# The order of the first 200 steps of a fused mLSTM and feed-forward kernel, rewritten

## The chip, the cores and the metric

One core of a Trainium2 chip runs the kernel. The metric is the device time of one execution in microseconds (us). The core has five engines that run side by side, each through its own list of instructions: PE (TensorE, matrix products), ScalarE (ACT in the profile), VectorE (DVE), GpSimd (POOL) and SyncE (SP), which here only issues DMAs.

## The reference

Two layers, one behind the other. The first is an mLSTM recurrence over 768 time steps for 4 batches and 8 heads of 40 channels; the second a feed-forward layer on the 3072 tokens.

```
for t in range(S):
    m_new = maximum(f[t] + m, i[t])
    f_stab, i_stab = exp(f[t] + m - m_new), exp(i[t] - m_new); m = m_new
    C = f_stab * C + i_stab * outer(v[t], k[t]);  n = f_stab * n + i_stab * k[t]
    y[t] = sigmoid(o[t]) * (C @ q[t]) / maximum(abs(n . q[t]), 1)
x = y as (3072, 320)
h = x @ w_in                                       # (3072, 2048)
g = where(h >= 1, h, where(h <= -1, 0, (h + 1)**2 / 4))
return g @ w_out                                   # (3072, 320)
```

## The kernel before

**Tiling.** The recurrence is computed in chunks of 128 time steps, 6 per batch, so 24 pieces numbered n = 0 to 23 (chunk n // 4, batch n % 4). Within a piece the recurrence is two matrix products per head: scores of k against q (`score.n`), multiplied by a 128x128 matrix of decays, then the product with the values (`main.n`). The state between chunks is made by `carry.n`. Four pieces give 512 tokens; for these the feed-forward layer runs in 16 blocks of 128 hidden channels: `mm` (x @ w_in, 8 matmuls of 512 columns), `relu`, `max`, then `out` (first blocks) or `outh` and `outl` into four PSUM sums, and `sto`.

**The order.** The whole program is a string, `STEPS` (line 48), read from left to right. Each word is one step of a kind with its number; a kind that is a generator goes on to its next yield each time it is named. Inside `STEPS` every instruction is tied to the one before it on the same engine, so the string is the order of each engine's instructions, SP's DMAs among them. What an engine doesn't wait for by its data it does in that order.

**The steps of the front.** They start the kernel before its streaming middle:

- `fi`, `fb`: DMAs of the gates: those of the first chunk, and two copies of those of chunks 1 to 4. `id`: the identity matrix (`ident`) and other constants. `cs`: a mask for `carry`.
- `sums.0`, `gtail.0`, `gex.0`: the gate sums of the first chunk on VectorE (tile `ac` and others, from `fi`), and one transposition on PE with exponentials on ScalarE (`G`).
- `mask.b`, `add.b`, `dec.b.h`: decays of the first chunk, batch b, made on PE: two 512-column matmuls write a mask into two PSUM banks, two groups of five add the sums, and ScalarE writes the exponentials of the two halves into the tile `Abc` (or `A`).
- `bmax.0` twice (a scan over 512 steps; then four DMAs that spread the maxima, `m_b<-m_r`), `bsum.0` three times, `btail.0` four times, `exps.0`, `decs.0` twice: the gates of chunks 1 to 4. `bsum.0`'s third part stores the sums to DRAM (`a_d`), from where `A.n` reads them back, spread over 128 partitions; `prep.n` then makes decays of them (POOL's selection, ScalarE's exponentials).
- `qk.n`: two DMAs of q and k (160 KB each). `vv.n`: values of two pieces (324 KB and a little more in tile `ow`); `v.n`, `qn.n`, `og.n`: values with k, q in another layout, output gates of a chunk. `v1.n`, `v2.n`: values times gates on POOL. `sig.n`: the sigmoid of the output gates on ScalarE, which loads another function table for it and back.
- `W.k`: DMA of the k-th piece of the weights, w_in (768 KB) and w_out (640 KB) in turn. `w.k`: its conversion, in five parts for w_in (ScalarE, ScalarE, VectorE, ScalarE, VectorE: tiles `mg`, `win`, `wh`, `wl`), three for w_out.
- `hot.k`: k matmuls of 512 columns on a tile of zeros, whose result nobody reads (filler).
- `score.n`: 16 passes on PE, then VectorE multiplies each half with the decays. `main.n` for n below 4: 16 passes (decayed scores times values), the denominators `z`, `y` times sigmoid, three transposes, two copies.

PSUM has eight banks of 512 columns, and the steps that need one take one that is free.

Setup ahead of `STEPS` (zeros, identity and mask in bf16) is the same in both versions.

Of the kernel before, what the change touches and what calls it, by code (L numbers as in the profile page):

```python
# [45 lines left out]


STEPS = (
    "fi.0 mask.1 fb.0 W.0 vv.0 mask.0 hot.2 sums.0 mask.3 qk.1 add.1 hot.2 add.0 qk.2 w.0 w.0 bmax.0 id.0 dec.1.0 "
    "dec.1.1 dec.0.0 score.1 qk.3 gtail.0 hot.2 hot.2 bmax.0 gex.0 score.1 mask.2 qk.0 add.2 dec.2.0 dec.2.1 vv.2 "  # L50
    "add.3 v.4 dec.3.1 v1.1 dec.3.0 score.1 og.0 W.1 dec.0.1 score.2 main.1 score.0 bsum.0 bsum.0 bsum.0 w.0 "
    "score.3 score.2 score.2 one.0 score.0 v.1 score.0 v1.2 btail.0 w.0 v1.0 sig.0 main.1 btail.0 hot.4 btail.0 "
    "btail.0 w.0 v1.3 main.0 score.3 v.0 main.0 W.2 hot.2 exps.0 main.0 main.1 main.2 hot.2 hot.2 qn.5 A.4 score.3 "
    "v2.4 main.2 main.2 main.0 w.1 v2.1 qk.4 main.0 w.1 cs.0 main.3 main.1 main.2 main.0 W.3 v.5 carry.4 main.3 "
    "main.3 hot.2 v2.0 qn.4 main.1 decs.0 main.1 v.2 w.1 carry.1 main.3 A.5 A.6 main.2 w.2 carry.0 main.2 main.3 "
    "main.3 prep.4 carry.0 w.2 v1.4 prep.4 v2.5 score.4 w.2 prep.4 decs.0 W.4 carry.1 w.3 -- score.4 mm.0 relu.0 "
    "max.0 mm.1 w.2 main.4 w.2 relu.1 main.4 W.5 carry.5 W.6 carry.4 v2.2 w.3 w.3 main.5 main.5 prep.5 prep.5 "
    "score.4 carry.2 carry.2 max.1 mm.3 relu.3 prep.5 mm.2 w.4 carry.5 qk.5 prep.6 main.4 relu.2 main.4 v1.5 max.3 "
    "w.4 w.4 carry.5 prep.6 w.5 qk.6 og.1 max.2 out.0 out.1 out.2 w.5 w.5 w.4 w.4 score.5 so.1 score.5 score.5 A.7 "
    "W.7 score.6 w.6 carry.4 carry.4 v.6 w.6 prep.7 score.6 prep.6 mm.5 w.6 score.6 v1.6 qn.6 sig.1 main.5 main.4 "  # L60
    "main.4 so.2 relu.5 so.2 max.5 main.5 mm.4 relu.4 w.6 main.5 w.6 qn.7 w.7 w.7 prep.7 out.3 main.6 main.6 main.6 "
    "v2.6 carry.6 max.4 mm.6 carry.5 w.7 gh.5 gl.5 carry.6 gh.4 so.3 so.3 v.3 v2.3 carry.3 W.8 outh.4.2.3 carry.6 "
    "w.8 w.8 mm.7 outh.4.0.1 gl.4 main.6 outl.4 outh.5.2.3 A.8 relu.6 carry.3 main.7 A.9 qk.7 score.7 w.8 main.5 "
# [965 lines left out]
```

## Time and profile before

| | |
|---|---|
| median of 3 runs | 466.06 us |
| the three runs | 465.94, 466.06, 479.42 us |
| the profiled execution, its own time | 465.84 us |
| its span in the profile | 464.1 us |
| PE busy | 456.0 us (98% of the span), 3333 matmuls |
| VectorE, ScalarE, POOL busy | 350.7, 327.5, 144.1 us |
| read and written in DRAM | 55.96 and 4.01 MB |

The span is the time from the first to the last instruction in the profile; 1.74 us of the execution's time lie around it. Times in the rows below count from the span's start. A matmul's duration is longer than the distance to the next one's start, because matmuls overlap; the distances tell what PE can do.

### The profile page before, as it was taken

How to read it: one execution, taken by the hardware profiler on the slowest of the kernel's cores; microseconds unless marked ns; L12 is line 12 of the kernel's file. 1: busy time of each engine (PE TensorE's matmuls, PEld its weight loads, DVE VectorE, ACT ScalarE, POOL GpSimd, SP SyncE). 2: the span in 40 equal slices, each digit the busy share in tenths (PEclk: the TensorE clock that was granted, in tenths of full speed). 3: DMA queues.
4: the chain of work that ended last, by engine and by line, in shares of the span. 5: the costliest groups of instructions: out<-in, count | busy, mean ns of one | idle time of the engine just before them, and what ended most of it. 6: DMA issues, size and time to landing. Idle time of an engine off the chain costs nothing.

```text
span 464.1 us, 8795 instructions
## 1 busy us (share of the span) xinstructions
PE 456.0 (98%) x3333; PEld 408.5 (88%) x3336; DVE 350.7 (76%) x625; ACT 327.5 (71%) x593; POOL 144.1 (31%) x153
## 2 busy tenths in 40 slices
PE   6999999999999999999999999999999999999996
PEld 3888789998899999999988899989988898989986
DVE  5786789998979889878999988786775985443523
ACT  3679999998985586877777666766777734464651
POOL 2364233212543624423425643433213231000000
PEclk9999999999999999999999999999999999999999
DMA  6899959726445442564165437234616000010001
GB/s 215 291 283 352 296 175 347 220 67 166 147 115 148 118 132 91 171 177 124 48 177 161 118 89 203 63 78 155 159 57 160 1 1 0 2 42 16 1 0 57
DMA packets 23048, 60.60 MB, mean 131 GB/s; under 512 B 2599, under 2 KB 9535, under 8 KB 23007
## 3 DMA queue, kind: packets, MB, share of 16 engines
q1 hardware_dynamic: 22719, 59.81, 43.2%
q8 instruction: 26, 0.43, 0.4%
q10 hardware_dynamic: 288, 0.25, 0.2%
q14 instruction: 15, 0.12, 0.1%
HBM read 55.96 MB, written 4.01 MB: 129 GB/s over the span
## 4 chain that ended last, share of the span: by engine, by line
PE 87%; DVE 4%; ACT 3%; DMA 3%; issue 1%; SPq 1%; DVEq 0%
PE ps L189 87%; DMA qs<-in_qs 1%; DMA ident<-in_cst 1%; ACT r L189 1%; DVE stk L189 1%; SPq L189 1%; DVE hv L189 1%; DVE r L189 1%; DVE gl L189 0%; ACT Abc L189 0%; ACT raw L189 0%; ACT win L189 0%; ACT mg L189 0%; DVE win L189 0%; DVE xl L189 0%
## 5 line engine op out<-in xcount | busy, mean ns | idle before, releaser
L189 PE MATMUL ps<-oh,gh 128*128 128x320 f32 x368 | 112.3, 315 | 0.1
L189 PE MATMUL ps<-ow,gh 128*128 128x320 f32 x368 | 110.1, 309 | 0.0
L189 PE MATMUL ps<-xh,wh 128*128 128x512 f32 x288 | 100.6, 403 | 0.1
L189 PE MATMUL ps<-xh,wl 128*128 128x512 f32 x288 | 98.2, 395 | 0.0
L189 ACT ACTIVATE r<-ps,half 128x512 f32<-128x512 f32 x96 | 65.6, 683 | 44.5 <-PE ps L189 39.4
L189 DVE SCALAR_TENSOR_TENSOR r<-ps,r 128x512 f32<-128x512 f32 x96 | 64.7, 685 | 39.0 <-ACT r L189 38.7
L189 DVE TENSOR_TENSOR gl<-r,gh 128x512 fp32r<-128x512 f32 x92 | 69.9, 769 | 25.7 <-ACT gh L189 24.7
L189 ACT CAST gh<-r 128x512 fp32r<-128x512 f32 x92 | 56.2, 617 | 46.4 <-PE ps L189 21.6
L189 PEld LDWEIGHTS ps<-oh,gh 128*128 128x128 f32 x368 | 69.1, 188 | 1.9 <-issue 0.3
L189 PEld LDWEIGHTS ps<-ow,gh 128*128 128x128 f32 x368 | 69.2, 188 | 1.3
L189 PE MATMUL ps<-oh,gl 128*128 128x320 f32 x368 | 70.2, 311 | 0.0
L189 PEld LDWEIGHTS ps<-xh,wl 128*128 128x128 f32 x288 | 54.1, 188 | 12.8
L189 ACT ACTIVATE r<-r 128x512 f32<-128x512 f32 x96 | 60.7, 633 | 3.0
L189 PE MATMUL ps<-xl,wh 128*128 128x512 f32 x192 | 60.3, 395 | 0.0
L189 PEld LDWEIGHTS ps<-oh,gl 128*128 128x128 f32 x368 | 58.1, 188 | 1.1
L189 PEld LDWEIGHTS ps<-xh,wh 128*128 128x128 f32 x288 | 50.3, 188 | 7.8 <-DVE Abc L189 0.2
L189 ACT ACTIVATE Abc<-Abc,nA 128x128 f32<-128x128 f32 x160 | 50.4, 391 | 0.1
L189 POOL TENSOR_TENSOR v<-vk,G 128x328 f32<-128x328 f32 x36 | 28.9, 807 | 53.2 <-DMA vk<-in_vk 28.2
L189 POOL TENSOR_TENSOR y<-y,z 128x320 f32<-128x320 f32 x24 | 21.1, 882 | 76.2 <-DVE y L189 76.2
L189 PEld LDWEIGHTS ps<-xl,wh 128*128 128x128 f32 x192 | 36.0, 188 | 8.8
L189 POOL TENSOR_TENSOR m<-m 128x1024 bf16<-128x1024 f32 x16 | 31.6, 1976 | 37.6 <-DVE m L189 35.0
L189 DVE SCALAR_TENSOR_TENSOR stk<-raw,ident,qs 120x1024 fp32r<-120x1024 f32 x28 | 37.9, 1356 | 2.9 <-ACT raw L189 2.8
(143 smaller groups left out, 665.4 us busy)
## 6 DMA issues: line engine op xcount, KB each, us to landing
qs<-in_qs SPq DMA_DIRECT2D x28, 480.0 KB
Abc<-a_d SPq DMA_DIRECT2D x20, 512.0 KB
vk<-in_vk SPq DMA_DIRECT2D x20, 324.0 KB
wraw<-in_w_in SPq DMA_DIRECT2D x8, 768.0 KB
wraw<-in_w_out SPq DMA_DIRECT2D x8, 640.0 KB
sig<-in_og SPq DMA_DIRECT2D x6, 640.0 KB
qn<-in_qn SPq DMA_DIRECT2D x20, 180.0 KB
raw<-in_qk SPq DMA_DIRECT2D x20, 160.0 KB
```

What stands on the lines that cost most here:

```text
L189: r = getattr(self.engine, name)(*args, **kwargs)
```

## The change

The first 204 words of `STEPS` are put into another order. They are the same words, each as often as before; from `mm.5` (near the end of the last changed line) both lists are the same. No function changes. In the new list `sums.0`, `gtail.0` and `add.1` come right behind the gate DMAs, `id.0`, `vv.0`, the first `bmax.0` and `qk.1` stand ahead of `W.0`; the other masks, the scores, the fillers and the loads behind them move with respect to each other.

```diff
 STEPS = (
-    "fi.0 mask.1 fb.0 W.0 vv.0 mask.0 hot.2 sums.0 mask.3 qk.1 add.1 hot.2 add.0 qk.2 w.0 w.0 bmax.0 id.0 dec.1.0 "
-    "dec.1.1 dec.0.0 score.1 qk.3 gtail.0 hot.2 hot.2 bmax.0 gex.0 score.1 mask.2 qk.0 add.2 dec.2.0 dec.2.1 vv.2 "
-    "add.3 v.4 dec.3.1 v1.1 dec.3.0 score.1 og.0 W.1 dec.0.1 score.2 main.1 score.0 bsum.0 bsum.0 bsum.0 w.0 "
-    "score.3 score.2 score.2 one.0 score.0 v.1 score.0 v1.2 btail.0 w.0 v1.0 sig.0 main.1 btail.0 hot.4 btail.0 "
-    "btail.0 w.0 v1.3 main.0 score.3 v.0 main.0 W.2 hot.2 exps.0 main.0 main.1 main.2 hot.2 hot.2 qn.5 A.4 score.3 "
-    "v2.4 main.2 main.2 main.0 w.1 v2.1 qk.4 main.0 w.1 cs.0 main.3 main.1 main.2 main.0 W.3 v.5 carry.4 main.3 "
...
+    "fi.0 mask.1 fb.0 sums.0 gtail.0 add.1 dec.1.0 dec.1.1 id.0 hot.2 vv.0 bmax.0 mask.3 mask.0 gex.0 qk.1 v1.1 W.0 "
+    "w.0 w.0 add.3 hot.2 one.0 score.1 score.1 add.0 dec.0.0 score.1 qk.0 w.0 w.0 dec.0.1 main.1 bmax.0 bsum.0 "
+    "score.0 score.0 v1.0 dec.3.1 mask.2 og.0 sig.0 hot.4 bsum.0 qk.3 score.0 main.0 qk.2 vv.2 v1.2 w.0 add.2 "
+    "dec.2.0 dec.2.1 main.1 main.0 score.3 W.1 bsum.0 W.2 score.2 main.1 dec.3.0 score.2 score.2 v1.3 qk.4 hot.2 "
+    "btail.0 hot.2 hot.2 main.2 main.0 hot.2 v.1 v2.1 score.3 main.0 score.3 v.0 btail.0 btail.0 cs.0 w.1 main.3 "
+    "w.1 w.1 v.2 score.4 carry.1 main.0 btail.0 decs.0 hot.2 main.3 main.1 w.2 w.2 main.2 main.2 v2.0 main.0 main.3 "
+    "main.1 v2.2 carry.1 A.4 prep.4 main.1 hot.2 main.2 main.2 carry.0 carry.0 exps.0 qn.5 v.4 main.2 v2.4 main.5 "
+    "qn.4 W.3 decs.0 main.5 main.3 main.3 A.5 prep.5 main.3 w.2 carry.2 v1.4 main.4 prep.4 score.4 prep.4 score.4 "
...
```

## Rows read from the trace of the kernel before

**Rows 1.** Busy us by windows: length, PE, PEld, VectorE, ScalarE, POOL, clock, DMA share, GB/s.

```profile
0.00:12.07 12.07, 8.11 (x49) 4.28 (x51) 7.21 (x24) 4.41 (x6) 3.10 (x15) 1.00 0.66 212
12.07:53.52 41.45, 41.30 (x330) 34.90 (x332) 30.52 (x68) 33.48 (x66) 17.61 (x22) 1.00 0.97 312
53.52:464.10 410.58, 406.63 (x2955) 369.35 (x2955) 312.95 (x535) 289.64 (x522) 123.36 (x117) 1.00 0.38 110
```

**Rows 2.** Timeline, PE: start us, us, engine, line, operation, out<-in, shape, count.

```profile
2.18 0.58 PE L186 MATMUL ps<-late_t,idb 128*128 128x512 bf16 x1 [2.18 <-POOL rst L186]
2.56 1.49 PE L189 MATMUL ps<-late_t,idb 128*128 128x512 bf16 x3
3.84 1.06 PE L189 MATMUL ps<-zeros 128*128 128x512 bf16 x2
...
5.59 0.39 PE L189 MATMUL ps<-ac,pick 96*128 96x128 bf16 x4
...
6.47 0.59 PE L189 MATMUL ps<-zeros 128*128 128x512 bf16 x2
...
9.02 0.46 PE L189 MATMUL ps<-raw 40*128 40x128 f32 x2 [1.07 <-DMA raw<-in_qk]
...
14.51 1.16 PE L189 MATMUL ps<-raw 40*128 40x128 f32 x16
15.60 1.98 PE L189 MATMUL ps<-ow,Abc 128*128 128x41 f32 x16
...
22.52 0.27 PE L189 MATMUL ps<-ident,fi_b 128*128 128x128 f32 x1
...
22.95 1.88 PE L189 MATMUL ps<-ow,Abc 128*128 128x41 f32 x16
24.66 1.03 PE L189 MATMUL ps<-zeros 128*128 128x512 bf16 x4
25.53 0.49 PE L189 MATMUL ps<-ident,y 128*128 128x128 f32 x3
...
53.52 0.70 PE L189 MATMUL ps<-xh,wh 128*128 128x512 f32 x2
```

**Rows 3.** Timeline, ScalarE, 6 to 24 us; in brackets the idle time before.

```profile
6.95 0.90 ACT L186 ACTIVATE mg<-wraw 128x768 f32<-128x768 f32 x1 [4.93 <-DMA wraw<-in_w_in]
...
8.53 1.55 ACT L189 ACTIVATE Abc<-ps 128x512 f32<-128x512 f32 x3
...
21.25 1.27 ACT L189 ACTIVATE sig<-sig 128x1280 f32<-128x1280 f32 x1 [1.68 <-DMA sig<-in_og]
22.54 1.28 ACT L189 ACT_TABLE_LOAD   x1
```

**Rows 4.** Timeline, VectorE, 9 to 18 us.

```profile
9.19 0.14 DVE L189 COPY carry<-m_r 32x1 f32<-32x1 f32 x1
11.01 1.29 DVE L189 TENSOR_TENSOR Abc<-ps,Abc 128x512 f32<-128x512 f32 x2 [1.67 <-PE ps L189]
14.75 0.62 DVE L189 TENSOR_TENSOR fi_b<-fi_b,m_b 128x128 f32<-128x128 f32 x2 [2.46 <-DMA m_b<-m_r]
...
16.45 0.95 DVE L189 SCALAR_TENSOR_TENSOR win<-mg,win 128x768 int32<-128x768 int32 x1
```

**Rows 5.** Timeline, DMA issues on SP, 0 to 24 us.

```profile
2.56 0.43 SPq L189 DMA_DIRECT2D wraw<-in_w_in  x1
...
7.98 3.37 SPq L189 DMA_DIRECT2D m_b<-m_r  x4
...
14.25 0.42 SPq L189 DMA_DIRECT2D sig<-in_og  x1
...
16.38 0.33 SPq L189 DMA_DIRECT2D a_d<-fi_r  x1
...
23.05 0.33 SPq L189 DMA_DIRECT2D Abc<-a_d  x1
```

**Rows 6.** Timeline, POOL, at 31 us: the selection of piece 4.

```profile
30.89 1.09 POOL L189 TENSOR_SCALAR_AFFINE_SELECT Abc<-Abc 128x1024 f32<-128x1024 f32 x1
```

10 rows, old and new, of the table STEPS are left out of this document.

## The prediction

> **What bounds the kernel now.** I read the page's busy shares first (PE 98%), then the busy time by windows cut where the changed part of the list ends. The first `mm.5` matmul, the first work behind the changed steps, starts at 53.52 us [rows 2]. In the 410.6 us from there PE is busy 406.6 us, and nothing in them is reordered; in 12.07 to 53.52 it is busy 41.30 of 41.45 us [rows 1]. So TensorE's own work sets the time, and the change can only alter how early PE reaches `mm.5`. The time that PE doesn't use lies almost wholly in the first 12.07 us, where it is busy 8.11 us, part of that at half speed [rows 1]. Next I read the timelines of that stretch engine by engine. They show three things. PE starts at 2.18 us, and its 512-column matmuls start 0.43 us apart up to about 5.2 us, against 0.22 us later: (3.84 - 2.56) / 3 against (25.53 - 24.66) / 4 [rows 2]. That is 1.2 and 2.4 GHz; the granted-clock column says 1.00 throughout and doesn't show it. Second, PE waits: `score.1` begins at 9.02 after 1.07 us for a piece of q and k that queues behind the first piece of w_in [rows 2]. Third, ScalarE runs the first two conversion steps from 6.95 before it makes the first decays at 8.53 [rows 3].
>
> **The yardstick.** After the same steps, `main.2` starts its first real product (call it up.2; up.0 and up.1 are those of batches 0 and 1). Up to it both lists hold the same PE steps (four masks, 14 filler matmuls, four `add`, four scores, `gex`, up.1, up.0), but the old list has `exps.0` as well. Old: up.2 starts at 22.95 and `exps.0` took 22.52 to 22.95 [rows 2], so the shared work was done at 22.52. The new list's start of up.2 minus 22.52 is the change, as long as nothing later stalls.
>
> **Removed.** Both lists start `add.1` at 5.59 us, since it hangs on the gate sums on VectorE, which are not moved. From there to 22.52 are 16.93 us. Prices by start-to-start [rows 2]: `add` 0.88 (5.59 to 6.47), a score 1.09 (14.51 to 15.60), an up 1.71 (22.95 to 24.66), a filler or half mask 0.22, a transpose 0.11 (four in 0.43). The old list's work in that stretch is 4 x 0.88 + 4 x 1.09 + 2 x 1.71 + 12 fillers and 2 half masks at 0.217 (3.04) + 0.11 = 14.45 us. So 2.48 us there are waits, and they are what the change can take away: w_in's piece no longer stands ahead of q and k, and the first decays no longer stand behind its conversion.
>
> **Added, part 1: work that loses its place.** While the gate sums run, old PE does eight matmuls (three masks and two fillers); the new list has only the two of `mask.1` ahead of `add.1`. Six matmuls move behind 5.59: 6 x 0.217 = +1.30 us.
>
> **Added, part 2: the clock.** Old PE works without a break from 2.18, and by 5.59 it runs at 2.4 GHz. New PE works from 2.18 to about 3.1 and then stands for 2.5 us. No row shows PE after such a break. I take it that the lower level lasts as long after 5.59 as it does in the one stretch that the trace has (2.18 to about 5.2), so to about 8.7. What runs until then, `add.1`, two fillers and half a mask, takes double: +0.88 + 0.43 + 0.21 = +1.52 us. The bounds are 0 (full speed from 5.59) and 3.0 us (a stretch twice as long); I take 1.52, from the nearest row.
>
> The Trainium skill ("TensorE: Matmul & The Clock Gate", Part 1: The HAM clock gate) says that the array idles at half rate, that activity lifts it, and that the point of the rise differs from run to run of one kernel. The trace agrees with half rate at the start; one profile can't show the spread. By that page the term may come out as nothing, and that is the first rival.
>
> **Added, part 3: two new gaps.** Step by step from 5.59: `add.1` to 7.35, fillers 8.20, `mask.3` 8.85, `mask.0` 9.28, `gex` 9.4, `add.3` 10.3, fillers 10.7, `score.1` 11.8, `add.0` 12.7. VectorE multiplies score 1 in two halves of 0.65 (11.01, [rows 4]), to 13.1, and only then can up.1 go: a gap of 0.4 us. up.1 to 14.8, `score.0` 15.9, `mask.2` 16.35, four fillers 17.2. VectorE multiplies score 0 from 15.95; the grid rounding of `bsum.0` (0.45) stands between its halves, so it ends at 17.7 and up.0 starts at 17.75: a gap of 0.55 us. up.0 to 19.45, `add.2` 20.35, `score.3` 21.45, `score.2` 22.5, six fillers 23.8, while VectorE finishes score 2 at 23.85. up.2 starts at 23.85. Gaps: +0.95 us.
>
> **What hides the rest.** SP: ident, the first value block and the first q and k pieces are issued ahead of w_in's first piece, which leaves some 2 us later than 2.56 [rows 5]. It took 4.4 us to land [rows 3, 5], so it lands at 9 to 10.2; its two ScalarE steps (1.6 us) then end at 11.9 at the latest, and VectorE takes it at 13.1 (0.95 us, [rows 4]): covered by 1.2 us. The four copies that broadcast the maxima start when the long scan ends. The same VectorE instructions end at 9.33 in the old list [rows 4] and about 9.2 in the new one, so the copies leave at 9.2 instead of 7.98 and, with no q and k landings to wait for between them, take some 2.1 us instead of 3.37 [rows 5]. The old ones landed 3.4 us after the last issue (11.35 to 14.75 [rows 4, 5]); the new ones so by 14.7. VectorE's `bsum.0` reaches them at 14.2 and is done (0.6 us) ahead of score 0 at 15.95: nothing, and 0.6 us of cover. The 2.46 us that VectorE waited there before [rows 4] were no wait of PE's.
>
> **Sum** against the profiled execution's 465.84 us: -2.48 + 1.30 + 1.52 + 0.95 = +1.3, so 467.1. The median of the three runs, 466.06, lies 0.22 above that execution; with this the time is 467.3 us, +0.3%. A measurement of this kernel tells about 2% (9.3 us) from no change; all of PE's unused time in the changed part is less than that.
>
> **Rival 1: the clock is up in time.** Without the 1.52 us the walk gives up.2 at about 22.35 (gaps 1.0 us): -0.2, so 465.7 to 465.9. If both gaps closed as well, 15.77 us of work from 5.59 would give -1.16: 464.7, which is the floor, since no work is removed. For it: 0.9 us of early work. Against: a break nearly three times as long.
>
> **Rival 2: loads come late behind the sums' store.** `a_d` is written when VectorE has scanned the sums: new at about 20.5 (behind up.0's `z` step), old at 16.38 [rows 5]. On SP everything else queues behind it: `W.2`, q and k 4, four value blocks, `A.4`. `A.4` also waits until `a_d` has landed, old 6.7 us (16.38 to 23.05), and POOL's selection began 7.8 us after that (30.89) [rows 5, 6]. With both durations kept, the selection comes at 35.0 and `v2.4` behind it on POOL at 36.1, where `carry.4` on PE wants it at 35.3: 23.85 plus 11.4 us (two ups, score 4, six steps of six passes at 0.107, twelve transposes and the four of `exps.0`, six fillers). `qn.5` behind `A.4` on SP is wanted at about 33. That is a stall of 1.5 to 3 us: 468.8 to 470.3. Against: at 20.5 the queue holds little besides `W.1`, where the old `a_d` stood behind five loads, so both durations should shrink by some 2 us. It decides once `a_d` takes over 5 us to land. DMA engines are 0.97 busy in this whole stretch [rows 1], so lost time there doesn't come back.
>
> **Rival 3, slower: ScalarE stuck at the sigmoid.** In the new list `sig.0` stands ahead of the decays of batch 2 and of half of batch 3. `og.0` leaves SP behind the maxima at about 11.3. With the old 7.0 us (14.25 to 21.25) it lands at 18.3; sigmoid 1.27, table load 1.28, decays 0.52 each [rows 3], so batch 2's first is done at 21.4 (`add.2` ends at 20.35), and VectorE wants it at 22.55. The cover is 1.1 us. From 8.1 us of landing time each further one goes to score 2, up.2 and PE. With the time of one more piece of w_in in the queue (4.4 us), it is 3.3 us: 470.6. Past 2% (475) it would need 10 us, or it would have to make ScalarE, which is busy 33.5 of the 41.5 us from 12.07 to 53.52 [rows 1], late in what follows.
>
> The same skill ("DMA: Bandwidth & Descriptors", Anatomy of one DMA) gives a fixed cost of about 2.0 us and 436 GB/s beyond it. By that, an estimate, `og.0`'s 0.64 MB land 3.5 us after issue and rival 3 is gone; the trace's 7.0 us stands against it, so I keep the rival.
>
> **Chances.** Forecast 0.50; rival 1 0.23; rival 2 0.17; rival 3 0.08, of it 0.03 past 2%; not named 0.02. The range 464.6 to 470.3 reaches from rival 1's floor to the top of rival 2. Faster by over 2%: 0.01, since PE's work stays; within 2%: 0.95; slower: 0.04.
>
> **What would show it.** In the new profile: PE's 512-column matmuls after 5.59 start 0.43 apart to about 8.7; `add.1` at 5.6; `score.1` without a wait for q and k; up.1 at 13.1, up.0 at 17.75, up.2 near 23.9 and `mm.5` near 54.8; VectorE without a long wait for the maxima; from 53.5 us on the same spacing as before. It is wrong if up.2 starts before 22.5 or after 25.5, if PE stands in 24 to 55 us, or if the part behind `mm.5` changes its length by over 1 us, for which I have no term.

## The result, and the profile after

| | before | after |
|---|---|---|
| median (lowest to highest), 4 runs each | 466.09 us (465.94 to 479.42) | 471.31 us (470.83 to 472.01) |
| profiled execution, its span | 465.84, 464.1 us | 470.83, 469.0 us |
| first matmul of `mm.5` | 53.52 us | 58.14 us |
| behind it | 410.58 us | 410.86 us |

The new list is slower: the ratio is 1.0115, with a 95% interval of [1.0098, 1.0133]. That is 5.2 us, above the forecast (467.3) and above the range (470.3). Against the bound of 2% it is still "no change". Executions more than 1.5% above the fastest of the same kernel, such as the one of 479.42 us, are left out of every ratio and of every count of falls here.

Busy time by windows, with the same cuts as in [rows 1] and the same columns:

```profile
0.00:12.07 12.07, 7.52 (x51) 4.28 (x52) 6.08 (x22) 4.02 (x6) 4.94 (x18) 1.00 0.62 188
12.07:58.14 46.07, 44.65 (x332) 37.20 (x332) 32.26 (x72) 34.25 (x67) 16.84 (x19) 0.93 0.93 292
58.14:469.00 410.86, 406.96 (x2957) 369.55 (x2955) 310.93 (x532) 289.49 (x522) 122.20 (x116) 1.00 0.37 109
```

4.62 of the 4.9 us by which the span grew lie ahead of `mm.5`, as they had to. The second window has what the one of before had not: 1.42 us in which PE isn't busy, and a mean granted clock of 0.93. PE's timeline shows where:

```profile
5.56 0.58 PE L189 MATMUL ps<-ac,pick 96*128 96x128 bf16 x4 [2.36 <-DVE ac L189]
...
7.22 1.06 PE L189 MATMUL ps<-zeros 128*128 128x512 bf16 x2
8.07 1.32 PE L189 MATMUL ps<-late_t,idb 128*128 128x512 bf16 x4
...
10.75 1.16 PE L189 MATMUL ps<-raw 40*128 40x128 f32 x16
...
12.81 1.95 PE L189 MATMUL ps<-ow,Abc 128*128 128x41 f32 x16
...
17.09 1.87 PE L189 MATMUL ps<-ow,Abc 128*128 128x41 f32 x16
...
23.07 1.88 PE L189 MATMUL ps<-ow,Abc 128*128 128x41 f32 x16
...
27.35 1.16 PE L189 MATMUL ps<-raw 40*128 40x128 f32 x16
29.61 1.58 PE L189 MATMUL ps<-ow 128*120 128x123 f32 x6 [1.10 <-POOL ow L189]
31.00 1.23 PE L189 MATMUL ps<-fi_r 128*120 128x16 f32 x6
...
35.01 1.26 PE L189 MATMUL ps<-ow 128*120 128x123 f32 x6
...
37.51 0.79 PE L189 MATMUL ps<-ow 128*120 128x123 f32 x6
...
39.36 0.72 PE L189 MATMUL ps<-xh,wh 128*128 128x512 f32 x2
```

The opening runs as it was walked through: `score.1` at 10.75 has no wait, up.1 is at 12.81, up.0 at 17.09, up.2 at 23.07. Then at 29.61 PE has stood (had nothing that it could start) for 1.10 us in front of `carry.1`, for a product on POOL; its idle time and what ended it stand in brackets. From there six matmuls on `ow` take 1.58 us, and six of the same shape 0.79 at 37.51. The windows around it say what that is (the granted clock is the third column from the right):

```profile
25.00:29.00 4.00, 3.52 (x37) 3.20 (x35) 3.22 (x15) 2.38 (x4) 0.17 (x1) 1.00 1.05 288
29.00:30.00 1.00, 0.39 (x2) 0.39 (x3) 0.57 (x2) 0.00 (x0) 1.00 (x2) 0.57 1.02 337
30.00:35.00 5.00, 4.78 (x21) 3.99 (x22) 1.24 (x3) 0.48 (x1) 1.61 (x3) 0.50 1.06 279
35.00:36.00 1.00, 1.00 (x6) 1.00 (x6) 0.32 (x2) 0.48 (x1) 1.00 (x3) 0.52 0.98 339
36.00:40.00 4.00, 4.00 (x37) 3.91 (x36) 3.35 (x8) 3.22 (x12) 1.82 (x3) 1.00 1.03 320
```

While PE stands, TensorE's clock falls to 1.2 GHz, and it stays there until about 36 us although PE is at work again. What PE stood for is read from the chain that ended last (start us, us, what):

```profile
19.40 0.04 DVE z L189
19.44 0.08 issue
19.52 0.37 DVE fi_r L189
19.89 0.19 DVE fi_b L189
20.09 0.17 SPq L189
...
21.58 7.18 DMA ow<-in_vk
...
28.83 0.74 POOL ow L189
...
29.61 3.04 PE ps L189 x13
```

Read backwards: `carry.1` waits for `v2.1` on POOL, that for the value block `v.1`, whose DMA took 7.18 us from 21.58. It left so late because it stands on SP behind the store `a_d`, which waits for VectorE's scan of the sums (19.52), and that stands behind up.0's `z`. In the old list the store leaves at 16.38 [rows 5] and `v.1` directly behind it, at 16.75.

**The balance.** Up to up.2 the new list loses 23.07 - 22.52 = 0.55 us. From up.2 to `mm.0` it takes 39.36 - 23.07 = 16.29 us; the same PE steps without any wait take 12.07 us (the kernel `g2_masks_too` below), so 4.22 are lost there: 1.10 of standing for the values and 3.1 behind it at the lower clock, 0.22 of these a second short idle time. 0.55 + 4.22 and -0.15 of small differences up to `mm.5` make 4.62; with 0.28 behind it, 4.9.

### The profile page after: what moved, and what is told of

Its sections match the earlier page's. It is cut to its first block, busy times and chain, and to the rows that moved or that the text cites. A ratio compares the mean times of both kernels' runs of the same rounds, so it can differ in the third digit from the quotient of the medians.

```text
span 469.0 us, 8796 instructions
## 1 busy us (share of the span) xinstructions
PE 459.1 (98%) x3333; PEld 411.0 (88%) x3336; DVE 349.3 (74%) x625; ACT 327.8 (70%) x593; POOL 144.0 (31%) x153
## 4 chain that ended last, share of the span: by engine, by line
PE 88%; DVE 5%; DMA 3%; ACT 1%; issue 1%; SPq 0%; POOL 0%; DVEq 0%
PE ps L189 88%; DMA ow<-in_vk 2%; DMA qs<-in_qs 1%; DVE stk L189 1%; ACT r L189 1%; DVE hv L189 1%; DVE r L189 1%; ACT raw L189 0%; DVE Abc L189 0%; DVE gl L189 0%; DMA fi<-in_fi 0%; DVE z L189 0%; SPq L189 0%; DVE xl L189 0%; ACT gh L189 0%
## 5 line engine op out<-in xcount | busy, mean ns | idle before, releaser
L189 POOL TENSOR_TENSOR v<-vk,G 128x328 f32<-128x328 f32 x36 | 30.3, 846 | 52.7 <-DMA vk<-in_vk 26.2
L189 POOL TENSOR_TENSOR y<-y,z 128x320 f32<-128x320 f32 x24 | 20.1, 839 | 73.8 <-DVE y L189 66.3
```

Source lines behind the costliest of these rows:

```text
L189: r = getattr(self.engine, name)(*args, **kwargs)
```

## The experiments

**Theory A:** the loads behind the store are late; PE stands for `v.1`; the stand lets the clock fall, and the fall costs more than the stand itself (3.1 us against 1.10 in this profile). **Theory B:** the late load itself is nearly all; the DMA engines are full in this stretch (0.97 busy, [rows 1]), so that one load sent earlier makes another late, and the clock is no cost of its own. Theories C and D are on the opening: that PE's early stand, or the six matmuls moved behind it, cost more than the 0.55 us of this profile. **Theory E:** the clock rises and falls by chance of the execution, whatever the list. What each gives for a kernel stands in its expectation, in the words of that moment. All lists have the same words as the new one, unless fillers are added; the ratios are to the kernel before, run beside them, and "a fall" is counted where an execution's mean granted clock is 0.996 or less. That mean is of the whole execution and doesn't tell where the clock was low; only the profiled execution of each list does.

| kernel | runs (of them left out) | median of all runs, us | ratio [95%] | falls |
|---|---|---|---|---|
| before, beside the lists below | 71 (7) | 466.06 to 466.26 | 1 | 11 of 64 |
| after; again as `g4_new_list_again` | 4; 4 | 471.31; 471.47 | 1.0115 [1.0098, 1.0133]; 1.0123 [1.0101, 1.0146] | 8 of 8 |
| `e1_values_early` | 12 | 468.49 | 1.0062 [1.0037, 1.0087] | 3 of 12 |
| `e2_fill_the_wait` | 6 (1) | 470.53 | 1.0090 [1.0068, 1.0111] | 0 of 5 |
| `e3_loads_early` | 6 | 469.4 | 1.0079 [1.0054, 1.0105] | 2 of 6 |
| `e4_masks_early` | 6 | 472.45 | 1.0113 [1.0067, 1.0159] | 4 of 6 |
| `f1_values_early_opening_filled` | 12 | 469.65 | 1.0078 [1.0046, 1.0110] | 8 of 12 |
| `f2_values_and_masks_early` | 12 (2) | 472.17 | 1.0084 [1.0047, 1.0121] | 6 of 10 |
| `f3_old_order_new_opening_loads` | 12 (8) | 478.74 | 1.0030 [1.0007, 1.0053] | 2 of 4 |
| `g1_loads_in_order_of_use` | 7 | 467.76 | 1.0034 [1.0022, 1.0046] | 0 of 7 |
| `g2_masks_too` | 12 | 468.18 | 1.0048 [1.0026, 1.0070] | 1 of 12 |
| `g3_before_with_late_values` | 12 (3) | 468.06 | 1.0033 [1.0007, 1.0059] | 4 of 9 |

**1. The late values sent early** (`e1_values_early`). Only SP's order changes.

```diff
-    main.0 score.3 W.1 bsum.0 W.2 ... main.0 hot.2 v.1 v2.1 score.3 main.0 score.3 v.0 btail.0
+    main.0 score.3 W.1 v.1 v.0 bsum.0 W.2 ... main.0 hot.2 v2.1 score.3 main.0 score.3 btail.0
```

> The changed kernel with the words v.1 and v.0 (DMAs of two value blocks) moved ahead of the third bsum.0, whose store of the sums SP has to wait for; nothing else. Theory A (the late landing of v.1 makes PE stand 1.1 us at carry.1, and that stand makes TensorE's clock fall to 1.2 GHz for 6.4 us): both go, the granted clock stays at 1.00 through 25 to 40 us, and of the 4.2 us lost between 28.45 and 39.36 us about 4 come back: 467 us against the changed kernel's 471.3. Theory B (the clock falls there because the new order leaves PE little to do in that stretch, wait or no wait): only the 1.1 us come back, 470 us, and the granted clock still shows 0.5 for some us. Theory C (the loss is that of the opening, where masks and fillers lost their place beside the gate sums): no change, 471.

PE's timeline of it:

```profile
24.04 1.87 PE L191 MATMUL ps<-ow,Abc 128*128 128x41 f32 x16
...
28.32 1.33 PE L191 MATMUL ps<-raw 40*128 40x128 f32 x16
29.58 0.89 PE L191 MATMUL ps<-ow 128*120 128x123 f32 x6
...
36.27 0.71 PE L191 MATMUL ps<-xh,wh 128*128 128x512 f32 x2
```

The stand is gone, the granted clock is 1.00 in all windows from 25 to 40 us, and up.2 to `mm.0` takes 12.23 us instead of 16.29: 4.06 of the 4.22 us are back in that stretch. The median gains less (2.8 us, so it misses the 467 of theory A), and in the profile up.2 itself is at 24.04, 0.97 later than in after, though not one of PE's steps ahead of it is changed: in this execution the matmuls were 0.43 us apart until about 10.5 us instead of 8.5. Theory A holds for the stretch. Three of twelve executions still show a fall, so chance has a part.

**2. The stand filled instead of removed** (`e2_fill_the_wait`). The load stays late; PE gets six matmuls on zeros to do in front of `carry.1`.

```diff
-    v.2 score.4 carry.1 main.0
+    v.2 score.4 hot.6 carry.1 main.0
```

> The changed kernel with six more filler matmuls (hot.6, 1.3 us at 2.4 GHz) directly ahead of the first carry.1, where PE stands 1.1 us for v.1's values; the load stays as late as it is. It adds PE work, so it could only help through the clock. Theory A: PE doesn't stand, the clock stays up, the three us that the lower clock cost between 29.6 and 36 come back, less 0.2 us by which the filler is longer than the wait: 468 us. Theory B: the clock falls all the same and the time is 471 to 472. Theory C: 471.5, the filler's surplus on top.

PE's timeline of it:

```profile
24.41 1.88 PE L191 MATMUL ps<-ow,Abc 128*128 128x41 f32 x16
...
30.14 1.24 PE L191 MATMUL ps<-zeros 128*128 128x512 bf16 x5 [0.16 <-issue]
31.30 0.89 PE L191 MATMUL ps<-ow 128*120 128x123 f32 x6
...
35.97 0.87 PE L191 MATMUL ps<-C,qn 120*128 120x123 f32 x6 [0.64 <-DMA qn<-in_qn]
...
39.29 0.72 PE L191 MATMUL ps<-xh,wh 128*128 128x512 f32 x2
```

The product on POOL that `carry.1` waits for:

```profile
30.51 0.74 POOL L191 TENSOR_TENSOR ow<-ow,G 128x328 f32<-128x328 f32 x1 [4.43 <-DMA ow<-in_vk]
```

PE is done with `score.4` at 29.98 and POOL with the product at 31.25, so the wait is still there, some 1.3 us, and the fillers fill it. With the load late as in after but PE at work, the clock doesn't fall in any of the five executions that are counted (0.999 to 1.000), against eight falls in eight of the unfilled list. This is what sets the stand apart from the load: the same six matmuls on `ow` take 0.89 us here and 1.58 in after. The median came 2.5 us above the 468 of theory A; the profile shows two reasons that make 2.2 of it: the opening's low stretch lasted to about 11.4 us (up.2 at 24.41, 1.34 later than in after), and PE, now earlier in its steps than the loads, stood for `qn` (0.64 and 0.19 us).

**3. All six loads ahead of the store** (`e3_loads_early`).

```diff
-    score.3 W.1 bsum.0 W.2 score.2 ... v1.3 qk.4 hot.2 ... v.1 v2.1 ... v.0 btail.0 btail.0 cs.0 w.1 main.3 w.1 w.1 v.2
+    score.3 W.1 W.2 qk.4 v.1 v.0 cs.0 v.2 bsum.0 score.2
```

> The changed kernel with six load steps (W.2, qk.4, v.1, v.0, cs.0, v.2) moved ahead of the third bsum.0, so that SP issues them in the 5 us in which it waited for VectorE's sums. Theory A: as with the two value blocks alone, 467, or up to 1 us better or worse, since the store of the sums and A.4 now queue behind 1.9 MB: if A.4 comes late, VectorE gets the decays of piece 4 late and PE stands ahead of main.4. Theory B: 470. Theory C: 471.

PE's timeline of it:

```profile
35.37 0.87 PE L191 MATMUL ps<-C,qn 120*128 120x123 f32 x6 [1.47 <-DMA qn<-in_qn]
```

The stand at `carry.1` is gone, and one of 1.47 us appears at 35.37, for `qn.5`, which comes behind `A.4` on SP. The clock stayed at 1.00 through that one, so a stand isn't always followed by a fall. The median of 469.4 misses theory A's 466 to 468 and lies near theory B's 470. So theory B is right in part: what stands ahead of the store pushes back what stands behind it.

**4. The masks put back ahead of the gate sums** (`e4_masks_early`).

```diff
-    fi.0 mask.1 fb.0 sums.0 gtail.0 add.1 dec.1.0 dec.1.1 id.0 hot.2 vv.0 bmax.0 mask.3 mask.0 gex.0
+    fi.0 mask.1 fb.0 mask.3 mask.0 hot.2 sums.0 gtail.0 add.1 dec.1.0 dec.1.1 id.0 vv.0 bmax.0 gex.0
```

> The changed kernel with mask.3, mask.0 and the first two fillers moved back ahead of the gate sums and add.1, as in the kernel before (six matmuls beside the gate sums); all loads stay in the new order. By the terms of the prediction, main.2's first product starts 1.3 us earlier for the work and up to 1.5 us earlier for the clock, at about 20.5 instead of 23.07 us, unless it is bounded by the sums. Theory C: the whole 2.6 us come back, 468.7. Theory A: the values of batch 1 follow the store of the sums, which comes as much earlier, so PE still stands at carry.1 and the clock still falls: 468.5 to 470 with the granted clock at 0.5 around 30 us. Theory B: the same with no wait needed.

PE's timeline of it:

```profile
2.56 2.34 PE L191 MATMUL ps<-late_t,idb 128*128 128x512 bf16 x5
...
5.55 0.63 PE L191 MATMUL ps<-ac,pick 96*128 96x128 bf16 x4
...
10.71 2.08 PE L191 MATMUL ps<-raw 40*128 40x128 f32 x16
...
17.81 2.08 PE L191 MATMUL ps<-raw 40*128 40x128 f32 x16
...
24.80 2.06 PE L191 MATMUL ps<-raw 40*128 40x128 f32 x32
...
28.10 1.88 PE L191 MATMUL ps<-ow,Abc 128*128 128x41 f32 x16
...
34.60 0.89 PE L191 MATMUL ps<-ow 128*120 128x123 f32 x6 [1.07 <-POOL ow L191]
```

The expectation failed. PE works from 2.18 us nearly without a break, and yet a score takes 2.08 us at 10.71 and at 17.81 and 1.03 at 24.80 (two in 2.06): the clock rose only at about 21 us, and up.2 came at 28.10. The execution at 468.39 us shows that it isn't always so. Early work doesn't guarantee an early rise, which speaks for theory E as to the opening. The stand at `carry.1` (1.07 us) and a fall behind it are here too.

**5. Values early, opening filled** (`f1_values_early_opening_filled`, `f2_values_and_masks_early`).

```diff
-    sums.0 gtail.0 add.1
+    sums.0 gtail.0 hot.6 add.1
```

> The kernel with v.1 and v.0 early, plus six filler matmuls (hot.6) ahead of add.1, where PE stands 2.4 us for the gate sums; at 1.2 GHz they take 2.56 us, so PE works from 2.18 us on without a break, as in the kernel before. Theory D (the clock rises late in the new order because PE stands there): TensorE's matmuls go to 0.22 us apart by about 5.5 us, as in the kernel before, instead of 8.5 to 11.4, up.2 starts near 21.7 us instead of 24.04, and the time is 466.0 to 466.6 against 468.4. Theory E (the moment of the rise differs from run to run and hardly with what PE does in its first 3 us): the rise stays anywhere between 5 and 20 us, the time 467.5 to 468.5 with the same spread of 5 us and more.

> The kernel with v.1 and v.0 early, plus mask.3, mask.0 and two fillers moved back beside the gate sums: the same PE work as before in the first 5.6 us, and the new order from add.1 on. Theory D: rise near 5.2 us, up.2 at 20.5 to 21 us, no wait at carry.1: 464.5 to 465.5, better than the kernel before. Theory E: the rise is as scattered as in the kernel with the masks early alone (to 21 us in its profile), 465 to 474 over the executions, median near 468.

The second has the edit of `e4_masks_early` in place of the fillers; both have that of `e1_values_early`. The first's profile:

```profile
22.28 1.87 PE L191 MATMUL ps<-ow,Abc 128*128 128x41 f32 x16
...
27.20 0.46 PE L191 MATMUL ps<-raw 40*128 40x128 f32 x2 [0.57 <-DMA raw<-in_qk]
28.17 1.16 PE L191 MATMUL ps<-raw 40*128 40x128 f32 x14 [0.51 <-DMA raw<-in_qk]
```

The clock was up at about 6.9 us and up.2 at 22.28, 0.24 ahead of the yardstick. But now `score.4` comes before its q and k, which still queue behind the store, and 8 of 12 executions show a fall, though the profiled one doesn't. In `f2_values_and_masks_early` these stands were 1.67 and 0.89 us, and the clock was at 0.50 from about 30 to 40 us in its profile (an execution of 474.01 us). The best executions of both are 466.4 to 467.4 us at a clock of 0.998 to 1.000; with a fall they take 469 to 473. None came to theory D's times: the first's best is 466.74 against 466.0 to 466.6, the second's 466.41 against 464.5 to 465.5. Of D's mechanism more is shown by the kernel before, profiled once more (`before_again`, 465.75 us): PE works there without a break from 2.19, and its matmuls are at full speed by 5.60 us, as in its first profile and as D had it; theory E had the moment over 1 us away.

**6. The loads in the order of their use** (`g1_loads_in_order_of_use`, `g2_masks_too`). The edit of the first is against `f1_values_early_opening_filled`, so it has the six fillers in the opening too; the second has the masks there instead.

```diff
-    score.3 W.1 v.1 v.0 bsum.0 W.2 score.2 ... v1.3 qk.4 hot.2 ... btail.0 cs.0 w.1 ... carry.0 exps.0 qn.5 v.4
+    score.3 W.1 qk.4 v.1 v.0 bsum.0 score.2 ... v1.3 hot.2 ... btail.0 qn.5 W.2 cs.0 w.1 ... carry.0 exps.0 v.4
```

> The new list with six filler matmuls ahead of add.1, and with q and k 4 and the value blocks 1 and 0 issued on SP ahead of the store a_d, and with qn.5 ahead of the second piece of w_in: the loads in the order in which PE wants them. Theory A (the loads behind the store make PE stand; the stand lets TensorE's clock fall): the kernel with only the values early and the same fillers took 467.4 us in its profiled execution and stood 1.08 us for q and k 4; without that, 466.3 us, no stand above 0.2 us between up.2 and mm.0, and the clock at 1.00 from 25 to 40 us. Theory B (the DMA engines are full, so one load earlier makes another late): a stand of 0.5 us or more for some other load (qn, W.2 by way of the conversion), 467 us or more. Theory E (the clock falls or rises late by chance, whatever the list): executions at 469 to 473 us as often as in that kernel (8 of 12).

> As the kernel before it, but in place of the six added fillers the two masks and two fillers that the old list has ahead of the gate sums' transposition are put there again, so that nothing is added. Theory A with the opening's clock: the kernel with values and masks early came to 466.4 us at best, with stands of 1.4 to 2.6 us for q and k 4 in its profile; without these 464.5 to 465.8 us at best, so below both kernels by 0 to 1.5 us. Theory B: the stand moves to the next load and the best stays at 466 us or above. Theory E: a part of the executions at 469 to 474 us all the same, so that the median is above 467 us.

The first, PE:

```profile
23.26 1.88 PE L191 MATMUL ps<-ow,Abc 128*128 128x41 f32 x16
...
34.75 0.87 PE L191 MATMUL ps<-C,qn 120*128 120x123 f32 x6 [0.49 <-ACT Abc L191]
...
36.05 0.71 PE L191 MATMUL ps<-xh,wh 128*128 128x512 f32 x2
...
54.97 0.87 PE L191 MATMUL ps<-xh,wh 128*128 128x512 f32 x2
```

PE shows no wait for a load, no execution of seven shows a fall, and all lie within 0.9 us (467.28 to 468.14). With that 3.7 of the 5.2 us are back. The list holds two edits, the loads and the opening's fillers; but up.2 is no earlier than in after (23.26 against 23.07), and up.2 to `mm.0` takes 12.79 us instead of 16.29, so in the profiles the gain lies behind up.2, where the loads are. The other 1.5 us show as 54.97 against 53.52 at `mm.5`: 0.74 by up.2 (0.24 of it a wait behind ScalarE's decays, and 0.5 in the two scores ahead of up.2, which take 2.51 us instead of 1.99; for what, the rows don't show) and 0.72 between up.2 and `mm.0` (0.49 of it a wait behind ScalarE's decays). My 466.3 was too low by these. The second kernel's best, 466.77 us, is no better than the kernel before, and its profile (471.54 us) is again one in which the clock rose only at about 21 us. It has no stand and no fall behind up.2, so that it gives the clean length of that stretch:

```profile
28.09 1.88 PE L191 MATMUL ps<-ow,Abc 128*128 128x41 f32 x16
...
33.46 0.89 PE L191 MATMUL ps<-ow 128*120 128x123 f32 x6
...
40.16 0.71 PE L191 MATMUL ps<-xh,wh 128*128 128x512 f32 x2
```

This list and `e4_masks_early` differ in the order of the loads alone, and their profiles have the same late opening (up.2 at 28.09 and 28.10). There the new order of the loads takes away a stand of 1.07 us and the fall behind it: up.2 to `mm.0` takes 12.07 us instead of 14.84 (28.10 to 42.94), the execution 471.54 us instead of 474.37, the median 468.18 instead of 472.45, with one fall in twelve instead of four in six. This is the test of the loads by themselves.

**7. The new list again** (`g4_new_list_again`).

> The new list unchanged, for the spread of its executions. Theory A: the stand of 1.1 us at carry.1 is there each time, so the clock falls behind it in nearly every execution: 470 to 472 us, none below 468.5. Theory E (the fall is chance): some executions at 467 to 468 us, as the kernel with the values early has 10 of 12 without the fall.

Four executions at 470.0 to 472.9 us, each with a fall; the profile has the stand again (0.88 us at 30.21) and 14.66 us from up.2 (23.89) to `mm.0` (38.55), 2.6 above the clean 12.07. With the first four that is eight of eight.

**8. Two runs from the side of the old list.** `g3_before_with_late_values` has one edit: `v.1` behind `qk.4`.

```diff
-    score.0 v.1 score.0 v1.2 ... qk.4 main.0 w.1 cs.0
+    score.0 score.0 v1.2 ... qk.4 main.0 w.1 v.1 cs.0
```

> The old list with one edit: the value block v.1 is issued behind q and k 4 instead of early, at about 24.5 us instead of 16.75, so it should land at 29.5 to 31.5 us and its product with the gates on POOL and PE's six matmuls on it, at 29.87 us before, come 1 to 2.5 us late. Everything ahead of that stays as in the kernel before, so this is the late load alone. Theory A (a stand of PE there lets the clock fall): the stand itself plus about 3 us, so 469 to 471 us in nearly all executions, with a stretch of some 6 us at half the clock behind it. Theory B (only the stand counts): 467 to 468.3 us at a clock of 1.00. Rival (POOL's work behind the values, the scaling of y, is what counts): PE stands at main's transposes first.

It didn't make the stand that it was built for: the store left at 15.21 us and `v.1` at 22.14 instead of 24.5, and POOL had it at 26.87 without a wait, so in the profile PE's steps stand as before (465.55 us). It shows that the old list has 5.4 us of room for this load and the new one none, but doesn't test stand and fall. Four of its nine counted executions fall (467.7 to 471.1 us), more often than in the kernel before (11 of 64), with no stand in its profile that would say why. `f3_old_order_new_opening_loads` is the old list with `id.0` behind `vv.0`, `W.0` behind `qk.1` and `dec.1.0`, `dec.1.1` ahead of the first `w.0`:

> The kernel before with the change's title alone: id.0 behind the first value block, W.0 behind the first q and k pieces, and the first two decays ahead of the first conversion steps; all the rest in the old order. By the prediction's first term PE's waits of 1.07 and 0.8 us at score.1 and 0.2 us at gex.0 go: 464.0 to 464.6, unless the next thing in line (VectorE's scores, the later piece of w_in) takes their place: then 465.5 to 466.1. If the granted clock or the rise shows a change here too, where no PE work is moved, theory E gains.

`score.1` starts at 8.78 without its wait, but w_in's piece lands only at 11.44, ScalarE stands 3.35 us for it with the next decays behind it, and PE stands 2.79 us ahead of `gex.0`. The profiled execution took 482.01 us, the fastest of twelve 466.83, so none came to the 464.0 to 466.1 expected. So the new order of the loads at the very front brought nothing in the old list: in this profile it trades a wait of 1.07 us for a longer one. The clock rose only at about 7.5 us, though PE's steps up to there are those of the kernel before, which speaks for theory E.

## Why the prediction was wrong

**Right, with the sizes.** `add.1` at 5.56 (5.59); low clock to about 8.5 (8.7); `score.1` without a wait at 10.75; w_in's piece taken by ScalarE at 10.81 (9 to 10.2, so 0.6 late) and by VectorE at 13.22 (13.1); the maxima's copies at 9.19 in 2.48 us (9.2, 2.1), and VectorE reached them at 14.15 without waiting; `a_d` at 19.92 (20.5); the part behind `mm.5` 0.28 us longer (none, bound 1). **Removed** and **Added, part 1** were not measured one by one; they and the clock's 1.52 give 0.34, and with the gaps that came (0.15) that is near the 0.55 us at up.2.

**Mis-sized: the gaps (part 3).** 0.95 us were forecast and about 0.15 came. I let up wait for both halves of VectorE's product; up.0 started at 17.09, while the second half ended at 17.63. PE begins with the heads of the first half.

**Mis-sized in another way: the clock (part 2).** In this profile 1.52 was right. But the five profiled executions that share these first steps saw the rise at 8.5, 10.1, 10.5, 11.4 and 11.4 us, with up.2 at 23.07 to 24.48. The loss in the opening is therefore 0.6 to 2.0 us, and that this profile shows the least of it is luck of the execution. My nearest row was one execution with unbroken work from 2.18 to 5.59. In nine profiled executions that have it (both of before, `e4_masks_early` and all of f and g but `g4_new_list_again`) the rise came by 7.5 us in seven and at about 21 in two, against 8.5 to 11.4 in the five with the stand. The sentence of the Trainium skill that I had beside it ("TensorE: Matmul & The Clock Gate", Part 1: The HAM clock gate: the point of the rise differs from run to run) agrees with these five numbers. I used it only for a rival on the favourable side.

**The step that failed** is the clause in the yardstick, "as long as nothing later stalls", with rival 2 at 0.17 and at a stall's price alone. The sum held no term behind up.2, where this profile lost 4.22 us: 1.10 of standing for `v.1` and 3.1 at the lower clock. Of the signs that were to show the forecast wrong, that one came (PE stands in 24 to 55 us); up.2 and the part behind `mm.5` stayed within theirs. Rival 2's mechanism is what happened: loads behind the sums' store. Two things in it were wrong. First the victim. I followed `A.4`, `v2.4` and `qn.5` and only named the "four value blocks"; `v.1`, wanted by `carry.1`, is due before all of them. The rows would have shown it, if only half its size: `a_d` at 20.5, then W.2 and q and k 4, gives `v.1` at about 22; with the 7.0 us that I had used for `og.0` and 0.74 on POOL it is ready at 29.8, where PE's steps from up.2 at 23.85 (up, two fillers, three transposes, up, score: 5.4 us) want it at 29.2. My own victims came to life only when the first was cured or filled: `qn.5` in `e2_fill_the_wait` and `e3_loads_early` (0.83 and 1.47 us), and the decays in `g1_loads_in_order_of_use` (0.49 us). The argument against, that durations shrink because the queue is short at 20.5, was half right: `A.4`, which waits for `a_d`, left 3.70 us behind it (19.92 to 23.62) and not 6.7, so the sign that was to decide, `a_d` taking over 5 us, did not come. But `v.1` took 7.18 us all the same. Second the price. I charged the clock for PE's break in the opening but for none behind it. 1.10 us of standing cost 3.1 us more, so rival 2's 1.5 to 3 us of stall should have reached beyond 470.3.

The Trainium skill has a sentence near to that which I hadn't weighed ("TensorE: Matmul & The Clock Gate", A second HAM failure mode: psum-queue depth-cycling): in one kernel PE's frequent short idle times between groups of matmuls made the clock go back and forth between its levels, at a cost. The trace agrees in that the clock fell behind a short idle time (0.50 in 30 to 35 us behind a stand of 1.10) and didn't where the stand was filled; but here it was one stand in a busy stream, which that section doesn't speak of.

**The rivals.** Rival 1 (clock up in time) did not occur; where the opening was filled and the clock up at 6.9, up.2 came at 22.28, so its -0.2 was the right size, and the loss went to the next load. Rival 3 did not occur: `og.0` left at 11.72 and the sigmoid began at 17.34 without a wait, so it had landed within 5.62 us. The 3.5 us that I had set beside it are from a section of the Trainium skill ("DMA: Bandwidth & Descriptors", Anatomy of one DMA) on DMAs that GpSimd issues; SP issues `og.0`, so the estimate did not bear on it.

**Open.** Why the list with a stand of 1.10 us fell in eight executions of eight, the one with two of about 0.5 us in eight of twelve (not in its profile), and why one of 1.47 us in the profile of `e3_loads_early` was followed by no fall. Over all lists whose profile has a stand of 0.5 us or more behind up.2 (after twice, e2 to f2), 28 of 47 counted executions fall; over those with none that long there (before, e1, g1 with its 0.49, g2, g3), 19 of 104. So a stand makes a fall likelier, and isn't the only thing that does. And what decides the clock's rise in the opening. Both vary between executions of one list; the runs show how often and what it costs, not by what it is set.

## What to carry to other kernels

When a list of steps is reordered, take every load that stands behind a moved store or wait on its queue, write down when its first user wants it, and begin with the one that is due first. Price a stand of TensorE at more than its length when nothing else keeps it at work: here 1.10 us cost 3.1 more and, in `g4_new_list_again`, 0.88 cost 1.7 more, while 1.47 us in `e3_loads_early` cost nothing more. Try fillers or an earlier load before touching the steps themselves. None of these lists beat the kernel before: an opening that is faster only brings PE to the next load sooner.

## What the runs showed of the hardware that I had not expected

- TensorE can stay at 1.2 GHz for long while it is fully busy. In `e4_masks_early` and `g2_masks_too` the matmuls were at half speed until about 21 us, with the granted clock printed as 1.00 there. The profiled execution of `f3_old_order_new_opening_loads` (482.01 us) fell behind its stand of 2.79 us (0.50 in 14.3 to 17.6 us), rose (0.98 in 17.6 to 21), and fell again shortly after 21 us though PE had no break. It stayed low to about 48 us, with a granted clock of 0.50 and PE busy 10.00 of 10.00 us in two windows running; what set off the second fall no run shows:

```profile
25.00:35.00 10.00, 10.00 (x44) 8.56 (x43) 4.66 (x15) 1.49 (x4) 2.10 (x3) 0.50 1.01 292
35.00:45.00 10.00, 10.00 (x46) 9.09 (x45) 4.54 (x13) 3.19 (x6) 5.12 (x6) 0.50 0.46 158
```

- With six matmuls on a tile of zeros in the place of a stand of 1.1 us the granted clock stayed at 0.999 or above, in all five executions that are counted.
- A value block (324 KB) took 7.18 us to land (21.58 to 28.76) while the DMA share was 1.01, with one piece of w_in and one of q and k ahead of it on its queue since the store; in the old list with the same block sent late (`g3_before_with_late_values`) it was there within 4.73 us (22.14 to 26.87), at the same DMA share.
